# A new place for the pool of W's rows, and a new place in the queue for later weight loads, in attention followed by two MLPs

## The chip, the cores and the metric

The kernel runs on one core of a Trainium2 chip. The metric is the device time of one execution in microseconds (us), the median over several runs. A core has TensorE for matmuls (PE in the profile, its weight loads are PEld), VectorE (DVE), ScalarE (ACT), GpSimd (POOL) and SyncE (SP). Each works through its own queue of instructions in order. Here SP issues all loads and nearly all stores, in the order of its queue, and POOL issues a few accumulating transfers.

## The reference

```python
# q, k, v: (2, 12, 448, 64), causal attention, then
x = attention.transpose(0, 2, 1, 3).reshape(896, 768)
h = ((x @ w1) * (x @ w2)) @ w3          # w1, w2: 768 x 1024, w3: 1024 x 1024
y = h @ w_out                           # w_out: 1024 x 768
z = np.maximum(y @ w_in2, 0.0) ** 2     # w_in2: 768 x 2048
return z @ w_out2                       # w_out2: 2048 x 768
```

The weights come as 64-bit floats: the kernel loads both 32-bit words of each and joins them to a float32 on the chip. q, k and v are float32.

## The kernel before

**Stages.** Twelve head pairs of attention run first. Between their steps TensorE also computes W = w3 @ w_out (both operands are known, so the product with h becomes one product with W), in eight row blocks of 128 x 768 in two passes (`w_half`). The tiles that hold these eight blocks are `wraw`, tagged W0 to W7, in the pool `attw`. When the second pass has added its part to a block (L430 or L434 on VectorE), SP stores it to the DRAM tensor `w_dram` (L620); the last store is that of W7. W is read back from there about 80 us later. Then come the products with w1 and w2, with W, and the second MLP, each by Strassen's method at one level with seven products in the order 1, 2, 6, 5, 7, 3, 4 for two pairs P and Q of weight blocks. One product is 9 matmuls of 128 x 448. Every operand is split into a high and a low float32r part: ScalarE casts the high one (L437), VectorE subtracts (L430).

**The blocks of x.** Attention's result gives seven block sums of x: B11 and B22 (kept in the long-lived pool `big`), B21, T4, T1, T2, T3. The last five are tiles of the pool `xt`, which opens when attention's pools close. Their parts are made in the order B21, T2, T1, T3, T4. Product 1 reads B11, product 2 B21, product 6 T2, product 5 T1, product 7 T3, product 3 B22, product 4 T4. In the profile's names, numbers are left out: xB is any of B11, B22, B21, and xT any of T1 to T4. After product 1 ScalarE copies its bank to a second one (`bank<-bank`), and product 2 goes on adding in the first, so product 2 of a pair waits for that copy of its own pair.

**Where tiles lie.** Pools lie one behind the other in SBUF in the order in which they are opened. Attention's pools, and what each takes per partition: `rawb` 6,144 bytes; `attq` 10,752 (three tiles of q and k); `attw` 24,576 (eight rows of 3,072); `ringb` 24,576 (four tiles of 6,144, parts of w_out); `attc` 22,784 (the identity 512, the mask 1,792, `pt_all` 12,288, two tiles of w3 of 4,096); `att` 20,864. When they close, `xt` and then `big2` are opened on the same bytes with `reuse_waits="tile"`: a new tile waits for whoever last used an old tile on its bytes. `xt` holds, from its start, P5 (3,072) and then B21, T4, T1, T2, T3 of 10,752 each. `big2` starts at byte 56,832 of the region.

**The order of the work.** Every operation is added to a `Program` with what it must come after (`after`), what it must only be issued behind (`behind`), and estimated times for its engine. `Program.order` plays these forward: each engine takes, among the operations that could begin first, the one that is due first. The resulting order is emitted as it is, each engine then runs its queue in order, and waits between engines are real semaphores. Loads are chained (`turn="loads"`), so they keep their own order.

**Weight loads.** `load_raw` adds a load into a raw buffer. Weights of w1 and w2 are 128 x 768 with two words (768 KB) and alternate between two raw buffers. A buffer is free again when three instructions have read it: `prelu` on ScalarE (L494), `lower` (L498) and `join` (L502) on VectorE. The keys in `order` are those of w3 and w_out; the first four other loads are w1's and w2's blocks 0 and 1, then blocks 2 of both, and so on.

Of the kernel before, what the change touches and what calls it, by code (L numbers as in the profile page):

```python
# [124 lines left out]
def attention_moe_moe2(ctx: ExitStack, tc: tile.TileContext, qk, v, w1, w2, w3, w_out, w_in2, w_out2, out):  # L125
    nc = tc.nc
    NP_ALL, P, S2 = qk.shape
    S = S2 // 2
# [19 lines left out]
    CLOSE = 4  # L148
    LENT = (("wout", 2), ("wout", 3))
    PAUSE = 64  # L150
    big = ctx.enter_context(tc.tile_pool(name="big", bufs=1))
    rawp = ctx.enter_context(tc.tile_pool(name="raw", bufs=2))
    ps_w = ctx.enter_context(tc.tile_pool(name="ps_w", bufs=2, space=PSUM))

    w_dram = tc.dram_tile([KF // 2, 2, P, DM], F32, name="w_dram")
# [15 lines left out]
    def mm(o, l, r, start, stop, **more):  # L171
        return nc.tensor.matmul(o, l, r, start=start, stop=stop, **more)  # L172
# [4 lines left out]
    def load(key, pool, tag, cols=None):  # L177
        src = source[key[0]][key[1]]
        n = src.shape[-1]
        if key not in raws:  # L180
            t = pool.tile([P, DM, 2], U32, tag=tag, name=f"raw_{key[0]}_{key[1]}")
            raws[key] = t[:, :n]
        x, src = raws[key], src.bitcast(U32)
        if cols is not None:
            x, src = x[:, cols], src[:, 2 * cols.start:2 * cols.stop]
        nc.sync.dma_start(out=x.rearrange("p f w -> p (f w)"), in_=src)
# [58 lines left out]
    def wide(u):  # L245
        return u[0] == "H"
# [32 lines left out]
    for u in units:  # L279
        key = u if wide(u) else u[1]  # L280
# [23 lines left out]
    loads = [it for it in items if it[0] in source]  # L304
# [5 lines left out]
    order = []  # L310
    for g in range(N3 // KF):
# [7 lines left out]
    attention = ExitStack()  # L319
    rawb = attention.enter_context(tc.tile_pool(name="rawb", bufs=1))  # L320
    attq = attention.enter_context(tc.tile_pool(name="attq", bufs=2))
    attw = attention.enter_context(tc.tile_pool(name="attw", bufs=1))
    ringb = attention.enter_context(tc.tile_pool(name="ringb", bufs=4))
    attc = attention.enter_context(tc.tile_pool(name="attc", bufs=1))
    att = attention.enter_context(tc.tile_pool(name="att", bufs=2))
    ps_a = attention.enter_context(tc.tile_pool(name="ps_a", bufs=6, space=PSUM))
    wraw = [attw.tile([P, DM], F32, tag=f"W{i}", name=f"wraw{i}") for i in range(KF)]
    ident = attc.tile([P, P], F32, tag="ident", name="ident")
# [5 lines left out]
        out=mask, in_=mask, compare_op=ALU.is_ge, fill=MASKED,  # L334
# [4 lines left out]
    prog = Program({"S": 700})  # L339
# [3 lines left out]
    def act(width, psum=False, strided=False):  # L343
        gap = 60 + 0.815 * width if psum else 75 + (0.96 if strided else 0.845) * width
        return {"A": (gap, gap + 105)}

    def dve(width, fast=False):
        gap = 70 + (0.52 if fast else 1.038) * width
        return {"V": (gap, gap + 85)}
# [79 lines left out]
    def tt(out, x, y, what):  # L429
        return lambda e: engine_of[e].tensor_tensor(out(), x(), y(), op=what)  # L430

    def negated(out, x, y, what):

        return lambda e: nc.vector.scalar_tensor_tensor(out(), x(), -1.0, y(), op0=ALU.mult, op1=what)  # L434

    def copy(out, x):
        return lambda e: engine_of[e].copy(out(), x()) if e == "A" else engine_of[e].tensor_copy(out(), x())  # L437
# [22 lines left out]
    def turn(what, n):  # L460

        count[what] += 1
        return (count[what] - 1) % n

    def load_raw(key, cols=None):

        if cols is not None and key in raw_place:
            place = raw_place[key]
        elif key in LENT:
            place = ("ringb", turn("lent", 4))  # L470
        elif key in order and turn("plain", RAW) == RAW - 1:
            place = ("rawb", 0)
        else:
            place = ("raw", turn("raw", 2))
        width = source[key[0]][key[1]].shape[-1]
        if cols is not None:
            raw_place[key] = place
            words = [place + (s, cols.start // HN) for s in "hl"]
            width = cols.stop - cols.start
        else:  # L480
            words = [place + (s, c) for s in "hl" for c in range(2)]
        size = width / DM
        pool, tag = {"raw": (rawp, "raw"), "rawb": (rawb, "rawb"), "ringb": (ringb, "ringb")}[place[0]]
        prog.add({"S": (2200 * size, 2500 + 2200 * size)}, lambda e: load(key, pool, tag, cols), [], words, turn="loads")
        return words[:len(words) // 2], words[len(words) // 2:]

    raw_place = {}

    def float32(key, words, width, y, names, cols=slice(None)):

        high, low = words

        def prelu(e):
            nc.scalar.activation(y(), raws[key][:, cols, 1].bitcast(F32), AF.Prelu, scale=2.0 ** -112, alpha=-2.0 ** 32)  # L494

        def lower(e):
            x = raws[key][:, cols, 0]
            nc.vector.tensor_scalar(x, x, 2.0 ** -29, 7.0, ALU.mult, ALU.min)  # L498

        def join(e):  # L500
            yi = y().bitcast(U32)
            nc.vector.scalar_tensor_tensor(  # L502
                yi, yi, 3, raws[key][:, cols, 0], op0=ALU.logical_shift_left, op1=ALU.bitwise_or)

        prog.add(act(width, strided=True), prelu, high, names)
        prog.add(dve(width, fast=True), lower, low, low)
        prog.add(dve(width), join, [*low, *names], names)
# [49 lines left out]
    def w_columns(f, c):  # L557

        if (f, c) in w_halves:
            return  # L560
        cols, row = slice(c * HN, (c + 1) * HN), 2 + f
        w_halves[f, c] = [("xs", row, c)]
        words = load_raw(("wout", f), cols)
        float32(("wout", f), words, HN, lambda: xs[:, row, cols], w_halves[f, c], cols)
# [9 lines left out]
    def w_parts(key):  # L574

        kind, n = key
        if kind == "w3":
            return [w3t[n][:, s] for s in range(2)]
        return ring_pair(2 * n) if n < NB else [hls[key][:, s] for s in range(2)]

    def w_half(g, i, n):
        n3, cols = g * KF + i, slice(n * HN, (n + 1) * HN)
        plain = n3 < PLAIN
        if plain:
            w_row(("w3", n3))
            for f in range(NB):
                w_columns(f, n)
        else:
            for key in order[:order.index(("w3", n3)) + 1] + [("wout", g * NB + f) for f in range(NB)]:
                w_row(key)  # L590
        place, acc = turn("w", 2), []
        reads = list(w_rows["w3", n3])
        for f in range(NB):
            reads += w_halves[f, n] if plain else w_rows["wout", g * NB + f]

        def run(e):
            acc.append(ps_w.tile([P, HN], F32, tag="w", name=f"w{n3}_{n}"))
            for f in range(NB):
                c = slice(f * P, (f + 1) * P)
                if plain:  # L600
                    mm(acc[0], w3t[n3][:, 0, c].bitcast(F32), xs[:, 2 + f, cols], f == 0, f == NB - 1)
                    continue
                t, wo = w_parts(("w3", n3)), w_parts(("wout", g * NB + f))
                for s, r in ((0, 0), (0, 1), (1, 0)):
                    mm(acc[0], t[s][:, c], wo[r][:, n],
                       f == 0 and (s, r) == (0, 0), f == NB - 1 and (s, r) == (1, 0))

        t0 = (3.72 if plain else 3) * NB * HN * PE_ROW + 100
        prog.add({"T": (t0, t0 + 170)}, run, reads, [("w", place)])
        dst = wraw[i][:, cols]  # L610
        if g == 0:
            prog.add(dve(HN) | act(HN, True), copy(lambda: dst, lambda: acc[0]), [("w", place)], [("wraw", i, n)])
            return
        if n == 0:
            add = negated(lambda: dst, lambda: acc[0], lambda: dst, ALU.subtract)
        else:
            add = tt(lambda: dst, lambda: acc[0], lambda: dst, ALU.add)
        prog.add(dve(HN), add, [("w", place), ("wraw", i, n)], [("wraw", i, n)])
        if n == 1:
            prog.add({"S": (1200, 3000)}, lambda e: nc.sync.dma_start(out=w_dram[i // 2, i % 2], in_=wraw[i]),  # L620
                     [("wraw", i, 0), ("wraw", i, 1)], [("wdram", i)])

# [206 lines left out]
    def fill(n=1):  # L831
        for _ in range(n):
            w_half(*w_units.pop(0))
# [59 lines left out]
    def slot_in(n, k):  # L893
        return {"T1": 0, "T3": KH, "T2": 2 * KH, "B21": 3 * KH}[n] + k

    for n in ("B21", "T2", "T1", "T3"):
        for k in range(KH):
            i = slot_in(n, k)
# [3 lines left out]
    for k in range(KH):  # L902
        i, b = slot_in("T2", k), slot_in("B21", k)
# [223 lines left out]
    def product(n, pair, unit, first_of_all):  # L1127
# [21 lines left out]
        def run(e):  # L1149
            o = bank(i)  # L1150
            if first_of_all:
                x = t[0][:, :P].bitcast(F32)
                mm(o[:, :PAUSE], x, x[:, :PAUSE], True, True)
            for k in range(KH):
# [285 lines left out]
```

## Time and profile before

| | us |
|---|---|
| median of 3 runs | 526.03 |
| lowest, highest | 525.83, 527.21 |
| the profiled execution, its own time | 526.13 |
| its span, first to last instruction | 524.4 |
| TensorE, VectorE, ScalarE busy in it | 511.9, 481.1, 396.0 |
| mean granted clock of TensorE | 0.995 of full speed |

The span is shorter than the time of the same execution, because the time also holds what lies around the first and the last instruction. All positions in the trace are counted from the span's start. A granted clock of 1.00 is 2.4 GHz, 0.50 is 1.2 GHz.

### The profile page before, as it was taken

How to read it: one execution, taken by the hardware profiler on the slowest of the kernel's cores; microseconds unless marked ns; L12 is line 12 of the kernel's file. 1: busy time of each engine (PE TensorE's matmuls, PEld its weight loads, DVE VectorE, ACT ScalarE, POOL GpSimd, SP SyncE). 2: the span in 40 equal slices, each digit the busy share in tenths (PEclk: the TensorE clock that was granted, in tenths of full speed). 3: DMA queues.
4: the chain of work that ended last, by engine and by line, in shares of the span. 5: the costliest groups of instructions: out<-in, count | busy, mean ns of one | idle time of the engine just before them, and what ended most of it. 6: DMA issues, size and time to landing. Idle time of an engine off the chain costs nothing.

```text
span 524.4 us, 8532 instructions
## 1 busy us (share of the span) xinstructions
PE 511.9 (98%) x2901; PEld 463.4 (88%) x2901; DVE 481.1 (92%) x1148; ACT 396.0 (76%) x977; POOL 16.0 (3%) x24
## 2 busy tenths in 40 slices
PE   6999999999998999999999999999999999999996
PEld 5768888888887999999999999999999999998996
DVE  4999999998888999999875899999999999999996
ACT  5898888776858574737576578998999589959971
POOL 1000000000000011221100000000000000000000
PEclk9999999999998999999999999999999999999999
DMA  8764635553570479999672311504540454035114
GB/s 311 281 218 164 222 141 175 168 162 114 200 239 3 164 225 258 278 259 229 139 223 93 121 60 56 187 1 156 173 154 1 151 184 147 2 131 177 55 60 151
DMA packets 27339, 81.68 MB, mean 156 GB/s; under 512 B 2464, under 2 KB 13472, under 8 KB 27296
## 3 DMA queue, kind: packets, MB, share of 16 engines
q1 hardware_dynamic: 23520, 75.64, 42.4%
q0 software_dynamic: 3776, 5.51, 6.4%
q8 instruction: 23, 0.38, 0.3%
q14 instruction: 20, 0.16, 0.1%
HBM read 75.24 MB, written 14.55 MB: 171 GB/s over the span
## 4 chain that ended last, share of the span: by engine, by line
PE 80%; DVE 11%; DMA 5%; ACT 3%; issue 1%; DVEq 0%
PE bank L172 59%; PE w L172 10%; PE s L172 4%; DVE ring L430 3%; PE x L172 3%; PE pp L742 2%; DVE g L430 2%; DVE xs L502 2%; DMA w_dram<-wraw 1%; DVE p L727 1%; DMA raw_w<-in_w 1%; DMA raw_wout<-in_w_out 1%; DMA raw_win<-in_w_in 1%; PE ph L760 1%; DVE xs L430 1%
## 5 line engine op out<-in xcount | busy, mean ns | idle before, releaser
L172 PE MATMUL bank<-xT,ring 128*128 128x448 f32 x630 | 132.1, 366 | 0.0
L437 ACT CAST ring<-xs 128x384 fp32r<-128x384 f32 (+1 forms) x194 | 102.4, 545 | 37.7 <-DVE xs L430 15.3
L172 PEld LDWEIGHTS bank<-xT,ring 128*128 128x128 f32 x630 | 117.8, 188 | 9.3 <-ACT bank L437 0.2
L430 DVE TENSOR_TENSOR ring<-xs,ring 128x384 fp32r<-128x384 f32 (+1 forms) x194 | 112.4, 596 | 11.9 <-ACT ring L437 11.4
L172 PE MATMUL bank<-xB,ring 128*128 128x448 f32 x489 | 104.5, 370 | 3.0 <-ACT bank L437 2.8
L172 PE MATMUL bank<-ring,g 128*128 128x384 f32 x600 | 105.0, 335 | 0.0
L172 PEld LDWEIGHTS bank<-ring,g 128*128 128x128 f32 x600 | 104.1, 188 | 0.4 <-ACT bank L437 0.2
L172 PEld LDWEIGHTS bank<-xB,ring 128*128 128x128 f32 x489 | 92.8, 190 | 11.5 <-ACT bank L437 3.2
L710 ACT ACTIVATE p<-p,st 128x320 f32<-128x320 f32 (+3 forms) x96 | 48.2, 517 | 8.4 <-DVE st L700 8.4
L430 DVE TENSOR_TENSOR xs<-xs 128x384 f32<-128x384 f32 x96 | 52.3, 557 | 0.2
L700 DVE CUSTOM_DVE_ANT_0 p<-s,mask 128x320 f32<-128x320 f32 (+3 forms) x96 | 35.1, 423 | 6.9 <-PE s L172 6.9
L437 ACT CAST g<-fs 128x384 fp32r<-128x384 f32 (+1 forms) x88 | 35.4, 416 | 7.8 <-DVE fs L430 7.6
L430 DVE TENSOR_TENSOR g<-fs,g 128x384 fp32r<-128x384 f32 (+1 forms) x88 | 37.1, 436 | 0.7 <-ACT g L437 0.5
L172 PE MATMUL w<-hl_wout,w 128*128 128x384 f32 x192 | 36.3, 341 | 0.0
L494 ACT ACTIVATE xs<-raw_w 128x768 f32<-128x768 f32 (+1 forms) x30 | 24.2, 811 | 13.2 <-DMA raw_w<-in_w 6.9
L172 PEld LDWEIGHTS w<-hl_wout,w 128*128 128x128 f32 x192 | 33.0, 188 | 0.6
L437 ACT COPY fs<-bank 128x448 f32<-128x448 f32 (+1 forms) x52 | 27.5, 529 | 6.7 <-PE bank L172 6.6
L172 PE MATMUL s<-qk 64*128 64x448 f32 (+3 forms) x192 | 28.1, 440 | 4.0 <-DMA qk<-in_qk 4.0
L172 PE MATMUL bank<-ab,ring 128*128 128x448 f32 x144 | 29.5, 365 | 0.0
L172 PEld LDWEIGHTS bank<-ab,ring 128*128 128x128 f32 x144 | 27.1, 188 | 2.1
L172 PEld LDWEIGHTS s<-qk 64*128 64x128 f32 x192 | 17.5, 208 | 12.3 <-issue 6.1
L172 PE MATMUL w<-ring,w 128*128 128x384 f32 x144 | 27.4, 341 | 0.2 <-DVE wraw L437 0.2
(84 smaller groups left out, 692.1 us busy)
## 6 DMA issues: line engine op xcount, KB each, us to landing
raw_wout<-in_w_out SPq DMA_DIRECT2D x20, 768.0 KB, 4.4
raw_w<-in_w SPq DMA_DIRECT2D x16, 768.0 KB, 5.1
raw_win<-in_w_in SPq DMA_DIRECT2D x16, 768.0 KB, 4.3
raw_w<-in_w SPq DMA_DIRECT2D x16, 512.0 KB, 3.6
qk<-in_qk SPq DMA_DIRECT2D x12, 448.0 KB, 5.3
s_dram<-w_dram POOLq DMA_DIRECT2D x8, 576.0 KB, 8.9
v<-in_v SPq DMA_DIRECT2D x12, 256.0 KB, 3.0
raw_wout<-in_w_out SPq DMA_DIRECT2D x8, 384.0 KB, 6.9
```

The lines of the kernel that those rows point to most:

```text
L172: return nc.tensor.matmul(o, l, r, start=start, stop=stop, **more)
L430: return lambda e: engine_of[e].tensor_tensor(out(), x(), y(), op=what)
L437: return lambda e: engine_of[e].copy(out(), x()) if e == "A" else engine_of[e].tensor_copy(out(), x())
L494: nc.scalar.activation(y(), raws[key][:, cols, 1].bitcast(F32), AF.Prelu, scale=2.0 ** -112, alpha=-2.0 ** 32)
L502: nc.vector.scalar_tensor_tensor(yi, yi, 3, raws[key][:, cols, 0], op0=ALU.logical_shift_left, op1=ALU.bitwise_or)
L700: prog.add({"V": (gap, gap + 160)}, lambda e: nc.vector.tensor_tensor_reduce(block(p, j, i), s_t[p, j, g][:, o:o + w], mask[:, S - w:], QS ...
L710: prog.add({"A": (gap, gap + 100)}, lambda e, i=i: nc.scalar.activation(block(p, j, i), block(p, j, i), AF.Exp, bias=st_t[p][:, 0, j, i:i ...
L727: lambda e, i=i: nc.vector.tensor_scalar(block(p, j, i), block(p, j, i), st_t[p][:, 3, j, i:i + 1], None, ALU.mult),
L742: nc.tensor.transpose(x[0][:, o:o + P], block(p, j, i)[:, c * P:(c + 1) * P], ident)
L760: nc.tensor.transpose(x[0][:SHORT, o:o + SHORT], block(p, j, c)[SHORT:, c * P:c * P + SHORT], ident[SHORT:, SHORT:])
```

## The change

`attw` is opened as the last of attention's pools instead of the third, so `ringb`, `attc` and `att` move down by its 24,576 bytes, and it lies behind them. And of the loads of weights that are not w3's or w_out's, those from the fifth on may only be issued behind the last store of W. The first four stay as free as they were. Nothing that is computed changes.

```diff
+    EARLY = 4
...
     attq = attention.enter_context(tc.tile_pool(name="attq", bufs=2))
-    attw = attention.enter_context(tc.tile_pool(name="attw", bufs=1))
     ringb = attention.enter_context(tc.tile_pool(name="ringb", bufs=4))
     attc = attention.enter_context(tc.tile_pool(name="attc", bufs=1))
     att = attention.enter_context(tc.tile_pool(name="att", bufs=2))
+
+    attw = attention.enter_context(tc.tile_pool(name="attw", bufs=1))
...
-        prog.add({"S": (2200 * size, 2500 + 2200 * size)}, lambda e: load(key, pool, tag, cols), [], words, turn="loads")
+        if key not in order:
+            later.append(key)
+        prog.add({"S": (2200 * size, 2500 + 2200 * size)}, lambda e: load(key, pool, tag, cols), [], words,
+                 behind=stored[-1:] if len(later) > EARLY else [], turn="loads")
...
+    stored, later = [], []
...
         if n == 1:
-            prog.add({"S": (1200, 3000)}, lambda e: nc.sync.dma_start(out=w_dram[i // 2, i % 2], in_=wraw[i]),
-                     [("wraw", i, 0), ("wraw", i, 1)], [("wdram", i)])
+            stored.append(prog.add(
+                {"S": (1200, 3000)}, lambda e: nc.sync.dma_start(out=w_dram[i // 2, i % 2], in_=wraw[i]),
+                [("wraw", i, 0), ("wraw", i, 1)], [("wdram", i)]))
```

All stores of W are added before the first load of w1, so `stored[-1:]` is always the store of W7.

## Rows read from the trace of the kernel before

**Rows 1.** The page's first line, and busy time by engine.
```profile
span 524.4 us, 8532 instructions
PE 511.9 (98%) x2901; PEld 463.4 (88%) x2901; DVE 481.1 (92%) x1148; ACT 396.0 (76%) x977; POOL 16.0 (3%) x24
```

**Rows 2.** Chain that ended last, in order of time: start, length, what.
```profile
151.18 6.81 DMA w_dram<-wraw
...
159.53 266.53 PE bank L172 x1353
```

**Rows 3.** TensorE in order of time, 149.5 to 200: start, length, what, idle before.
```profile
150.27 1.95 PE L172 MATMUL x<-pt_all,v 128*64 128x448 f32 x16
...
152.60 4.10 PE L172 MATMUL bank<-xB,ring 128*128 128x448 f32 x19
159.53 5.48 PE L172 MATMUL bank<-xB,ring 128*128 128x448 f32 x18 [2.83 <-ACT bank L437]
164.84 11.11 PE L172 MATMUL bank<-xT,ring 128*128 128x448 f32 x54
175.79 3.81 PE L172 MATMUL bank<-xB,ring 128*128 128x448 f32 x18
```

**Rows 4.** ScalarE in order of time, 149.5 to 161.
```profile
152.70 1.50 ACT L437 CAST xB<-fs 128x448 fp32r<-128x448 f32 x3
158.01 1.03 ACT L437 CAST xT<-fs 128x448 fp32r<-128x448 f32 x2 [3.81 <-DMA w_dram<-wraw]
158.95 0.52 ACT L437 COPY bank<-bank 128x448 f32<-128x448 f32 x1
```

**Rows 5.** Windows of 1 us: length, PE, PEld, DVE, ACT, POOL; clock; DMA share, GB/s.
```profile
157.00:158.00 1.00, 0.00 (x0) 0.00 (x0) 0.00 (x0) 0.00 (x0) 0.00 (x0) 1.00 0.07 28
...
160.00:161.00 1.00, 1.00 (x5) 0.91 (x5) 1.00 (x2) 1.00 (x3) 0.00 (x0) 0.76 0.00 0
161.00:162.00 1.00, 1.00 (x4) 0.87 (x4) 0.82 (x3) 1.00 (x3) 0.00 (x0) 0.50 0.00 0
162.00:163.00 1.00, 1.00 (x5) 0.87 (x4) 1.00 (x3) 1.00 (x3) 0.00 (x0) 0.50 0.00 0
163.00:164.00 1.00, 1.00 (x4) 0.91 (x3) 1.00 (x3) 1.00 (x4) 0.00 (x0) 0.54 0.02 8
164.00:165.00 1.00, 1.00 (x6) 0.93 (x6) 1.00 (x4) 1.00 (x4) 0.00 (x0) 1.00 0.00 0
```

**Rows 6.** VectorE in order of time, 149.5 to 161.
```profile
150.60 0.55 DVE L430 TENSOR_TENSOR wraw<-w,wraw 128x384 f32<-128x384 f32 x1
...
153.87 1.69 DVE L430 TENSOR_TENSOR xB<-fs,xB 128x448 fp32r<-128x448 f32 x3
158.61 1.16 DVE L430 TENSOR_TENSOR xT<-fs,xT 128x448 fp32r<-128x448 f32 x2 [3.04 <-ACT xT L437]
```

**Rows 7.** SP's issues in order of time, 143 to 180.
```profile
146.43 4.13 SPq L186 DMA_DIRECT2D raw_w<-in_w  x2
151.18 0.33 SPq L620 DMA_DIRECT2D w_dram<-wraw  x1
173.29 2.82 SPq L186 DMA_DIRECT2D raw_w<-in_w  x2
```

**Rows 8.** Landing of the two loads issued at 146.4 and 150.2, by tile.
```profile
DMA to landing us min/median/max: 6.1/6.4/6.8
```

**Rows 9.** Landing of the first seven stores of W, by tile.
```profile
DMA to landing us min/median/max: 2.3/2.9/4.7
```

**Rows 10.** ScalarE in order of time, 163 to 178: its next reads of a raw buffer.
```profile
164.79 0.91 ACT L494 ACTIVATE xs<-raw_w 128x768 f32<-128x768 f32 x1
...
170.36 0.92 ACT L494 ACTIVATE xs<-raw_w 128x768 f32<-128x768 f32 x1
```

**Rows 11.** Windows as in rows 5, the stages after attention.
```profile
160.00:200.00 40.00, 40.00 (x191) 36.92 (x191) 39.08 (x73) 28.65 (x56) 1.72 (x2) 0.96 0.49 154
...
250.00:300.00 50.00, 50.00 (x248) 46.35 (x247) 37.54 (x57) 30.88 (x52) 2.08 (x2) 1.00 0.51 147
```

## The prediction, made before the changed kernel was run

> **What bounds the kernel now.** I read the page first: TensorE is busy for 98% of the span [rows 1], so a change can only pay where TensorE stands still or runs slowly. Then the chain that ended last, because it names the places where something else has the lead. One such place lies just where attention ends: the chain goes through the last store of W, and from 159.53 on through TensorE alone for 266.53 us [rows 2]. So whatever moves TensorE's start at 159.53 moves 266 us of work behind it. Third, the engines one by one around that place. TensorE ends P's and Q's product 1 at 152.60 + 4.10 = 156.70 and stands idle for 2.83 us, until ScalarE's copy of a bank [rows 3]. That copy isn't late by itself: on ScalarE it stands behind two casts of T2, and these waited 3.81 us for the store of W7 [rows 4]. B21's three casts just ahead did not wait. Last, windows of one microsecond. After the idle stretch the granted clock falls to 0.76, 0.50, 0.50, 0.54 between 160 and 164 and is back at 1.00 after it [rows 5]; 0.50 is the 1.2 GHz level.
>
> **Why a cast of x waits for a store of W.** This comes from the sizes of the pools. Before, `attw` begins at 6,144 + 10,752 = 16,896, so W6 and W7 take bytes 35,328 to 41,472. In `xt`, T2 begins at 3,072 + 3 x 10,752 = 35,328. T2's first bytes are thus those of W6 and W7, and T2 is the first of the T blocks that is made. The trace agrees: the casts that wait are the first xT ones, and they start 0.02 us after the store landed at 151.18 + 6.81 = 157.99 [rows 2, 4].
>
> **Part one, the pool.** After the change, the region reads: `rawb` to 6,144, `attq` to 16,896, `ringb` to 41,472, `attc` to 64,256, `att` to 85,120, `attw` to 109,696. T2 (35,328 to 46,080) then covers the last `ringb` tile, the identity, the mask and 2,304 bytes of `pt_all`. Of these `pt_all` is used longest: by attention's last matmuls, which end at 150.27 + 1.95 = 152.22 [rows 3]. ScalarE is done with B21 only at 152.70 + 1.50 = 154.20 [rows 4]. So the new wait is over 2 us before ScalarE could start anyway; its price is zero, and it would count only if those matmuls ended after 154.2. T3 covers `pt_all` and the start of a w3 tile, T1 and T4 mostly `ringb`: all of them are read by TensorE ahead of 152.22 too. W's rows now lie under `big2`, at 85,120 - 56,832 = 28,288 and up within it, behind its first 7,168 and 21,504 bytes. What is written there are results of later products, of w2 among them, tens of us after the store has landed. I price that at zero too.
>
> **What TensorE gets.** In rows 4 the first bank copy starts 0.94 us after the first T2 cast. From 154.20 that gives 155.14, and with its 0.52 us the copy is done at 155.66, a microsecond before 156.70. The 2.83 us go. VectorE follows: it ends B21's low parts at 153.87 + 1.69 = 155.56 and can go on with T2 at once, where it waited for 3.04 us [rows 6]. Three low parts at about 0.6 us are done by 157.4, and T2 is wanted only after two more products, at about 156.70 + 3.64 = 160.3. No new wait there.
>
> The clock is the second term. The 18 matmuls from 159.53 took 5.48 us; the 18 of the same form at 175.79 took 3.81 [rows 3]. That is 1.67 us, and the windows give the same another way: 0.24 + 0.50 + 0.50 + 0.46 = 1.70 [rows 5]. In this trace the fall comes right behind the idle stretch, so I take it to go with it; its lower bound is zero, if the fall had another cause.
>
> **Part two, the loads.** Two loads, the fifth and sixth of w1 and w2, are issued at 146.43 and 150.2, ahead of the store at 151.18 [rows 7]. Now they are issued behind it, at about 151.5 and 151.9; their buffers are free by then. The store waits in SP's queue for VectorE's last sum, which ends at 151.15 [rows 6], so it is not issued earlier than now. But it no longer has 1.5 MB ahead of it: it lands after something like the other seven's 2.3 to 4.7 us [rows 9] instead of 6.81. With part one nobody waits for it, so this is worth nothing by itself. It is a second cure for the same stall.
>
> The cost: the loads land later. Together they and the store are the same three transfers as before, of which none took longer than 6.8 us [rows 2, 8]; so at most about 158.7. ScalarE reads them at 164.79 and 170.36 [rows 10], which become 160.3 and 165.9 if all moves by 4.5. The cover is 1.6 us for the first and 7 for the second. From above, if store and loads ran strictly one after the other, 4.7 + 6.8 = 11.5 us would put the first at 163.0, and ScalarE would stand for 2.7 us in front of copies out of banks. I take the nearer row, the same three transfers, and price it at zero. SP has nothing else queued until 173.29 [rows 7], so no other transfer is held up, and no load of attention is touched.
>
> The planner sees one new edge. Loads five and six are planned some 6 us later, still ahead of the moment when their data is taken; so I expect the same order on TensorE, VectorE and ScalarE, and on SP three transfers in another order.
>
> The Trainium skill speaks against this part: in "DMA: Bandwidth & Descriptors", section "Rules for kernel authors", it says to issue a transfer early and to wait for it late. By it the loads moved behind the store lose 5 and 2 us of lead, and the sum would fall by whatever of that is not covered. The rows give 1.6 us of cover at the tightest place, so here the rule would cost nothing.
>
> **Sum.** -2.83 - 1.67 + 0 + 0 = -4.50 us. The profiled execution took 526.13 us, 1.73 more than its span; 526.13 - 4.50 = 521.63. It lies 0.10 above the median of the runs, so I forecast **521.5**. Does it last to the end? Behind 159.53 TensorE never waits until 426, and VectorE and the loads take their pace from TensorE by way of buffers; VectorE has 12.5 us of idle time between 250 and 300 to fall in step [rows 11].
>
> **Rivals.** *VectorE keeps the rest.* It is busy for 39.08 of 40 us after 160 [rows 11], and it gains only 3.05 us (158.61 to 155.56) against TensorE's 4.50. If TensorE has less than 1.45 us of lead to spare over VectorE's data, the gain is 3.05: 523.0. Against it: TensorE shows no wait for VectorE there, even where it comes back to full clock. 8%.
>
> *The clock falls anyway*, since the cause was not the idle stretch: -2.83, 523.2. Against it is only the order of events. 5%.
>
> *The pool doesn't move T2 off W*, because tiles are not placed in the order I read from the code. Then part two decides. The store lands at 153.5 to 155.9 by rows 9; TensorE starts 1.52 us after it (158.01 to 159.53), so it idles for 0 to 0.7 us: 521.5 to 522.2. The skill's rule on completion (the same page, "Queues, rings and completion order": a transfer's semaphore is written only after every earlier write of that DMA engine) agrees with 6.81 against 2.3 to 4.7 and would by itself move the store the same way. 5%.
>
> *No change*, if some tile other than W7 ends T2's wait equally late, such as a load still landing under it: 526.0. I see none in the sizes. 3%.
>
> *Slower: the fifth load comes late.* ScalarE waits in order at its read, and copies out of banks stand behind it. Each microsecond past 160.3 costs TensorE at most one. To lose more than the gain and 1.6 us besides it would have to land after 166.4, 15 us after its issue; the longest of the two was 6.8 [rows 8]. At 12 us it would only eat 3 of the 4.5. If the planner also puts other work behind it, 528. 3%.
>
> **How the numbers follow.** The forecast holds 76%; its own spread is some 0.7 us, from the margins above. The two cases at 523.0 and 523.2 and the late load that eats part of the gain set the upper end, 523.3; below, the gain cannot be much over 4.5, and 520.7 allows for small shifts in the order behind. A measurement of this kernel tells 0.3%, 1.6 us, from no change. Faster: 76 + 8 + 5 + 5 = 94, of which I leave 1 for what I don't see: 93%. Within 0.3%: 4%. Slower: 3%.
>
> **What would show it.** Right: the first xT cast starts at about 154.2 with no wait for the store; TensorE has no gap at 156.70 and the clock stays at 1.00 through 165; T2's first product starts at about 160.3 instead of 164.84; the store is issued ahead of both loads and lands within 4.7 us; the chain no longer holds `w_dram<-wraw`. Wrong: a wait of ScalarE for `raw_w` near 160, a gap of TensorE that VectorE ends between 160 and 200, or a gain at 165 that is gone again by 426.

## The result, and the profile after

The changed kernel takes 522.05 us (median of 6 runs, 521.29 to 522.85); the kernel before took 526.59 in the same comparison (6 runs). The ratio is 0.991, with a 95% interval of 0.989 to 0.9931. 4.54 us were gained where 4.50 had been worked out, and 522.05 lies within the range given. The profiled execution of the changed kernel is the longest of its six, 522.85; the last section tells of a reason.

In the page, the span is shorter by 3.4 us and the work of the engines is the same:
```profile
span 521.0 us, 8529 instructions
PE 511.3 (98%) x2901; PEld 461.7 (89%) x2901; DVE 481.4 (92%) x1148; ACT 395.8 (76%) x977; POOL 15.9 (3%) x24
```
In the chain that ended last, nothing stands any more between attention's last matmuls and TensorE's own long stretch. The store of W, 6.81 us of the chain before [rows 2], is gone from it:
```profile
149.81 1.88 PE x L173 x16
151.69 281.88 PE bank L173 x1428
```
TensorE and then ScalarE in order of time. All starts in this execution lie about 0.5 us earlier already ahead of the place in question (152.06 against 152.60), so distances count:
```profile
152.06 7.75 PE L173 MATMUL bank<-xB,ring 128*128 128x448 f32 x37
159.65 11.11 PE L173 MATMUL bank<-xT,ring 128*128 128x448 f32 x54
```
```profile
152.16 1.50 ACT L439 CAST xB<-fs 128x448 fp32r<-128x448 f32 x3
153.56 1.04 ACT L439 CAST xT<-fs 128x448 fp32r<-128x448 f32 x2
154.50 0.53 ACT L439 COPY bank<-bank 128x448 f32<-128x448 f32 x1
...
160.35 0.90 ACT L501 ACTIVATE xs<-raw_w 128x768 f32<-128x768 f32 x1
...
165.17 0.92 ACT L501 ACTIVATE xs<-raw_w 128x768 f32<-128x768 f32 x1
```
The two groups of 19 and 18 matmuls of [rows 3] have become one of 37 without a gap. T2's first product starts 159.65 - 152.06 = 7.59 us behind the start of that group; before, it was 164.84 - 152.60 = 12.24. So 4.65 us are gained at this place: 1.66 because the 18 matmuls ahead of T2 take 3.65 us instead of 5.31 (159.53 to 164.84), and 2.99 because the first of them no longer stands. That is 0.16 more than the idle time of 2.83 in the row, which counts from the modelled end of the matmul before it. T2's casts follow B21's directly, with no wait behind them, and the bank copy starts 0.94 us after the first of them, as in [rows 4].

Windows of 1 us, columns as in [rows 5]. The clock stays at full speed:
```profile
157.00:158.00 1.00, 1.00 (x6) 0.93 (x5) 1.00 (x3) 1.00 (x3) 0.00 (x0) 1.00 0.14 55
160.00:161.00 1.00, 1.00 (x7) 0.93 (x6) 1.00 (x3) 1.00 (x3) 0.00 (x0) 1.00 0.00 0
161.00:162.00 1.00, 1.00 (x7) 0.93 (x6) 1.00 (x3) 1.00 (x3) 0.00 (x0) 1.00 0.00 0
```
SP's issues, then the landing of the store of W7 and of the two loads behind it. Two stores follow each other (145.03 and, 5.6 us later, 150.63), and the loads come behind:
```profile
145.03 5.93 SPq L628 DMA_DIRECT2D w_dram<-wraw  x2
151.06 27.46 SPq L187 DMA_DIRECT2D raw_w<-in_w  x6
```
```profile
DMA to landing us min/median/max: 2.6/2.6/2.6
```
```profile
DMA to landing us min/median/max: 5.0/5.7/6.3
```
The store lands at 153.25 instead of 157.99, and the loads at 156.03 and 157.88, some 4.3 and 7.3 us ahead of ScalarE's reads at 160.35 and 165.17.

### The profile page after: what moved, and what is told of

Read it like the earlier page. It is cut to its first block, busy times and chain, and to the rows that moved or that the text cites. A ratio compares the mean times of both kernels' runs of the same rounds, so it can differ in the third digit from the quotient of the medians.

```text
span 521.0 us, 8529 instructions
## 1 busy us (share of the span) xinstructions
PE 511.3 (98%) x2901; PEld 461.7 (89%) x2901; DVE 481.4 (92%) x1148; ACT 395.8 (76%) x977; POOL 15.9 (3%) x24
## 4 chain that ended last, share of the span: by engine, by line
PE 87%; DVE 7%; ACT 4%; DMA 2%; issue 0%; DVEq 0%
PE bank L173 62%; PE w L173 13%; PE s L173 4%; PE x L173 4%; PE pp L750 3%; DVE ring L432 2%; DVE g L432 2%; ACT p L718 2%; PE ph L768 1%; DMA raw_win<-in_w_in 1%; DVE xs L509 1%; DMA qk<-in_qk 1%; DVE xs L432 1%; ACT ring L439 0%; ACT g L439 0%; DVE p L735 0%
## 5 line engine op out<-in xcount | busy, mean ns | idle before, releaser
L173 PE MATMUL bank<-xB,ring 128*128 128x448 f32 x489 | 103.3, 367 | 0.2
L173 PEld LDWEIGHTS bank<-xB,ring 128*128 128x128 f32 x489 | 91.5, 188 | 8.8 <-DVE ring L432 0.5
```

## The experiments

The theory: T2 lies over W6 and W7, so T2's casts wait for the store of W7, and TensorE idles and slows down behind them. Either part of the change ends that, and the loads behind the store cost nothing as long as their cover lasts. The rivals: the order of the loads alone does it, or the pool alone; the slow clock has another cause; loads issued later cost time.

| run | median us | before, same comparison | ratio, 95% interval | from the first xB group to the first xT product, us |
|---|---|---|---|---|
| again (changed kernel) | 523.30 | 527.34 | 0.9917, 0.9894 to 0.9940 | 7.58 |
| pool_only | 522.36 | 527.34 | 0.9904, 0.9889 to 0.9919 | 7.58 |
| loads_only | 521.99 | 527.34 | 0.9905, 0.9886 to 0.9925 | 7.59 |
| rows_reversed | 521.66 | 527.34 | 0.9893, 0.9879 to 0.9906 | 7.59 |
| filler | 525.98 | 527.05 | 0.9973, 0.9946 to 0.9999 | 10.45 |
| pad_before | 530.83 | 527.05 | 1.0076, 1.0049 to 1.0103 | 14.91 |
| pad_after | 521.90 | 527.05 | 0.9928, 0.9901 to 0.9954 | 7.58 |
| pad_pool | 522.29 | 526.65 | 0.9921, 0.9891 to 0.9951 | 7.59 |
| early2 | 527.78 | 527.05 | 1.0024, 1.0001 to 1.0046 | 10.12 |
| early3 | 526.79 | 526.65 | 0.9992, 0.9972 to 1.0011 | 7.59 |

The last column is from each run's own trace: the start of TensorE's first `xT` row less that of the row that begins at 152.60 in [rows 3], where the kernel before has 12.24.

**again.** The changed kernel once more.

> The changed kernel once more. Theory: 4.5 us under the kernel before (about 522.1 against 526.6), TensorE without a gap between 156 and 160, clock 1.00 there. On the slower matmul cadence that the changed kernel's profile shows between 233 and 326 (207 ns from start to start against 203 in the kernel before): if it belongs to one execution, its place or length differs here; if it belongs to the program, it comes at the same place.

The gain repeats: 4.0 us between the medians, and 7.58 us at the place in question. The slower cadence came at another place, so its place belongs to the execution; see the last section.

**pool_only.** The pool moved, the loads left as they were.
```diff
-    attw = attention.enter_context(tc.tile_pool(name="attw", bufs=1))
     ringb = attention.enter_context(tc.tile_pool(name="ringb", bufs=4))
...
+    attw = attention.enter_context(tc.tile_pool(name="attw", bufs=1))
     ps_a = attention.enter_context(tc.tile_pool(name="ps_a", bufs=6, space=PSUM))
```


> The pool of W's rows laid out last, the loads as before. Theory (T2's bytes were those of W7): the store still lands some 6.8 us after its issue, behind both loads, but no cast waits for it; TensorE has no gap; the whole gain, about 522.1. Rival (the order of the loads is what cures): the gap of 2.8 us and the low clock stay, 526.6.

The landing of W7's store and ScalarE in order of time:
```profile
DMA to landing us min/median/max: 6.9/6.9/6.9
```
```profile
152.31 1.50 ACT L437 CAST xB<-fs 128x448 fp32r<-128x448 f32 x3
153.72 1.04 ACT L437 CAST xT<-fs 128x448 fp32r<-128x448 f32 x2
```
The store is as slow as before, and T2's casts start 4 us ahead of its landing at 157.7. So the wait was one for bytes, and the pool alone gives the whole gain.

**loads_only.** The loads behind the store, the pool left in third place (the second hunk of the change alone).

> The loads behind the last store, the pool where it was. Theory: T2 still waits for the store of W7, but the store lands 2.3 to 4.7 us after its issue at about 151, at 153.3 to 155.9, and ScalarE is free for T2 at about 154; TensorE loses 0 to 0.7 us: 522.1 to 522.8. Rival (the pool alone cures): the cast waits as long as before, 526.6.

```profile
DMA to landing us min/median/max: 2.6/2.6/2.6
```
```profile
152.67 1.50 ACT L438 CAST xB<-fs 128x448 fp32r<-128x448 f32 x3
154.07 1.04 ACT L438 CAST xT<-fs 128x448 fp32r<-128x448 f32 x2
```
T2 still lies over W7, but the store was issued at 151.14 and landed at 153.70, 0.37 us before ScalarE was free for T2. This too gives the whole gain, with 0.37 us to spare at the casts. The two parts are two cures of one stall; the gain is not their sum. The Trainium skill's "DMA: Bandwidth & Descriptors", section "Queues, rings and completion order", says that a transfer's semaphore is written only after every earlier write of that DMA engine; the trace agrees, with 2.6 us for the store ahead of the loads and 6.9 behind them, though it doesn't single this cause out.

**rows_reversed.** The kernel before, with the row tiles of W laid out in reverse.
```diff
-    wraw = [attw.tile([P, DM], F32, tag=f"W{i}", name=f"wraw{i}") for i in range(KF)]
+    wraw = [attw.tile([P, DM], F32, tag=f"W{i}", name=f"wraw{i}") for i in reversed(range(KF))][::-1]
```


> The pool where it was, the loads as before, but the eight row tiles of W laid out in reverse, so that T2 lies over W0 and W1, stored some 45 us earlier, and T4 over W7 and W6. T4 is made last, some 11 us behind T2. Theory (single tiles matter): no wait, about 522.1. Rival (new tiles wait for the whole pool of W's rows, or the place of that pool is what counts): 526.6.

The landing of the store of W7:
```profile
DMA to landing us min/median/max: 6.6/6.6/6.6
```
521.66 us: neither pool nor loads have moved, the store, issued at 150.71, still lands only at 157.35, and the gain is there. So what counts is which row lies under T2, not the place of the pool. W7 and W6 now lie under T4, which is made some 10 us later than T2: its first cast starts at 163.01, after the landing.

**filler.** The stall is kept, and TensorE gets something to do in it.
```diff
+    FILL = 14
...
+    def filler(unit, i):
+        def run(e):
+            for _ in range(FILL):
+                mm(bank(i), hls[unit][0][:, :P], xB["B11"][:, 0, 0], True, True)
+
+        prog.add({"T": (0, 0)}, run)
...
+        if at == 2:
+            filler(plan[0][3][0], free_banks[1])
         if kind == "product":
```


> The kernel before, with 14 extra matmuls of 128 x 448 into a bank that nobody uses yet, between Q's product 1 and P's product 2 (their result is never read). They fill TensorE's idle 2.83 us at about 0.2 us each and leave the wait as it is. Theory (the clock falls because of the idle stretch): the clock stays at 1.00 behind it and the 18 matmuls take 3.8 us instead of 5.5, so 1.7 us less than before, about 524.9. Rival (the clock falls for another reason): 526.6 or a little more.

ScalarE, TensorE, and one window:
```profile
157.79 1.04 ACT L438 CAST xT<-fs 128x448 fp32r<-128x448 f32 x2 [3.57 <-DMA w_dram<-wraw]
```
```profile
152.61 10.61 PE L173 MATMUL bank<-xB,ring 128*128 128x448 f32 x51
163.06 11.10 PE L173 MATMUL bank<-xT,ring 128*128 128x448 f32 x54
```
```profile
161.00:162.00 1.00, 1.00 (x6) 0.87 (x6) 0.82 (x2) 1.00 (x4) 0.00 (x0) 1.00 0.00 0
```
The wait for the store is there as before, TensorE has no gap, and the clock, 0.50 in this window before [rows 5], is 1.00. The distance to T2's product falls from 12.24 to 10.45 us, by 1.79. Of this the 18 matmuls ahead of it are 1.63: they take 3.68 us from start to start instead of 5.31, with 1.67 to 1.70 forecast. The rest goes with the store, which landed 0.2 us earlier in this execution, so that ScalarE waited for 3.57 us instead of 3.81. The medians differ by 1.1 us with an interval of 0.05 to 2.8, which holds it without pinning it down. What remains to 7.59, 2.86 us, is the time of the 14 extra matmuls.

The clocks of all executions say more than the medians. The four windows of [rows 5] lack 1.70 us at full clock, 0.003 of the span; so an execution with this fall can't show a mean granted clock above 0.997. Of the kernel before's 63 executions in the three later comparisons, 28 show 0.998 or more: these did not have it, or not in full. Of filler's 12 all show 0.998 or more. In the comparison with filler, the 18 of the kernel before with 0.998 or more have a median of 526.12 us, close to filler's 525.98; the other 17 have 528.06. So the fall goes with the idle stretch, but at most 35 of the 63 executions with that stretch paid for it.

**pad_before.** The kernel before, with one more load ahead of the last store.
```diff
+    padp = attention.enter_context(tc.tile_pool(name="padp", bufs=1))
...
+    def store(i):
+        if i == KF - 1:
+            pad = padp.tile([P, 1024], U32, tag="pad", name="pad")
+            nc.sync.dma_start(out=pad, in_=w2[KF - 1].bitcast(U32)[:, :1024])
+        nc.sync.dma_start(out=w_dram[i // 2, i % 2], in_=wraw[i])
...
-            prog.add({"S": (1200, 3000)}, lambda e: nc.sync.dma_start(out=w_dram[i // 2, i % 2], in_=wraw[i]),
+            prog.add({"S": (1200, 3000)}, lambda e: store(i),
```


> The kernel before with one more load of 512 KB, into a tile that nobody reads, issued just ahead of the store of W7. Theory: the store lands later by about 2 us (512 KB at the 250 GB/s of the loads around it), T2's casts and TensorE with it: 528 to 529. Rival (the store's landing isn't what TensorE waits for): 526.6.

ScalarE and TensorE:
```profile
159.72 1.03 ACT L438 CAST xT<-fs 128x448 fp32r<-128x448 f32 x2 [5.79 <-DMA w_dram<-wraw]
```
```profile
161.23 6.17 PE L172 MATMUL bank<-xB,ring 128*128 128x448 f32 x18 [4.81 <-ACT bank L438]
...
218.88 2.09 PE L172 MATMUL bank<-xB,ring 128*128 128x448 f32 x9 [1.05 <-ACT bank L438]
```
The store takes 8.8 us, TensorE's stall grows by 1.98 us and the slow matmuls behind it by 0.69: 2.67 at this place; the 2 expected had left the clock's part out. The median is 3.8 above the kernel before, where 1.4 to 2.4 were expected; the second row shows another wait, 1.05 us at 218.88, which the kernel before does not have there. All 12 executions show a mean granted clock of 0.997 or less, where the kernel before has such clocks in 17 of 35; if the longer stall is always followed by the fall, that is another part of the difference.

**pad_after.** The changed kernel with the same extra load.

> The changed kernel with the same extra load of 512 KB just ahead of the store of W7. Theory: the store lands later and nobody waits for it, and the fifth load lands later by about 2 us, against the cover of 1.6 at its read by ScalarE as it was forecast (4.3 as the changed kernel's profile has it): 522.1, at most 522.6. Rival (TensorE still hangs on the store): 523.5 or more.

521.90, but this run was no test: with loads five and six out of the way, SP came to the extra load at 145.67, and it landed at 150.27, before the store was issued. The store took 2.6 us as without it.

**pad_pool.** The test that this was meant to be, on pool_only.

> The pool of W's rows last, the loads as before, and the same extra load of 512 KB just ahead of the store of W7, now behind the fifth and sixth load as in the run of the kernel before with it (in the changed kernel with it, the extra load went out 5 us earlier and landed before the store was issued). Theory: the store lands at about 159.7 as there, and nobody waits for it: TensorE has no gap, 522.1 to 522.6. Rival (TensorE still hangs on the store): 528 or more.

The landing of the store, and ScalarE:
```profile
DMA to landing us min/median/max: 9.4/9.4/9.4
```
```profile
152.70 1.50 ACT L438 CAST xB<-fs 128x448 fp32r<-128x448 f32 x3
154.10 1.03 ACT L438 CAST xT<-fs 128x448 fp32r<-128x448 f32 x2
```
The store lands at 160.6, later than ever, 6.5 us after the casts that used to wait for it, and the kernel takes 522.29 us. The next transfer that reads `w_dram` is issued at 179.10 (sums made within DRAM), so the late landing delays nobody there either. What cost 3.8 us over the old layout costs nothing over the new one.

**early2.** Four loads behind the store instead of two (`EARLY = 2`).

> The changed kernel with EARLY = 2: the third and fourth load of w1 and w2 also go behind the last store. They then land at about 156 to 158 instead of 140 and 147, and product 6 needs sums of what they bring at about 159.6. Theory (loads behind the store are free only as long as their cover lasts): ScalarE waits for raw_w, TensorE waits 1 to 4 us before product 6, and 1 to 5 us of the gain are given back: 523 to 527. Rival (the place of loads in the queue doesn't matter here): 522.1.

TensorE in order of time:
```profile
161.69 11.78 PE L173 MATMUL bank<-xT,ring 128*128 128x448 f32 x54 [2.37 <-ACT ring L439]
...
238.26 5.49 PE L173 MATMUL bank<-xB,ring 128*128 128x448 f32 x18 [2.19 <-ACT bank L439]
```
The whole gain is gone, and a little more: 527.78. Product 6 waits 2.37 us for its sums. ScalarE did not wait for `raw_w`, as had been expected: its reads at 156.33 and 158.52 follow the work before them directly, and it is VectorE that is behind, busy for 4.96 of the 5 us from 157 with what the late loads bring among other work. Another wait of 2.19 us, with slow matmuls behind it, comes 77 us later.

**early3.** Only the fourth load joins the two (`EARLY = 3`).

> The changed kernel with EARLY = 3: only the fourth load joins those behind the last store. It brings Q's second block, whose sums product 6 of Q needs one product later than P's, at about 161.5. Theory: it lands at about 155, its chain on VectorE (lower, join, two sums, low part, some 3.5 us among other work) ends at about 160 to 162: 0 to 1.5 us given back there, 522.1 to 523.6. Rival (any of the first four loads behind the store costs as much as two of them): 527 to 528.

```profile
162.91 9.59 PE L173 MATMUL bank<-xT,ring 128*128 128x448 f32 x45 [0.92 <-ACT ring L439]
...
210.58 2.08 PE L173 MATMUL bank<-xB,ring 128*128 128x448 f32 x9 [1.40 <-ACT bank L439]
213.45 2.12 PE L173 MATMUL bank<-xB,ring 128*128 128x448 f32 x9 [0.79 <-ACT bank L439]
```
526.79, nearly as much as early2 and not the 522.1 to 523.6 expected. The wait at the place itself is 0.92 us, as worked out; but two more of 2.2 us together follow at 210, where the changed kernel's profile shows none above 0.1 and its repeat 0.6 together. VectorE, busy for 18.00 of 18 and 20.00 of 20 us from 157 to 195 in this run, can't make up work that starts later; but it is as busy in the changed kernel, 18.00 and 19.82. Its order differs in this run too, because the planner knows of the late load. And in this trace the slower cadence of the last section runs from about 214 to 338, some 600 matmuls at 4 ns, or 2.4 us beside the 3.1 us of waits. How much of the loss is backlog, order or cadence stays open.

With both runs, the rival of late loads is real, and the limit lies between the fourth load and the fifth. The Trainium skill's rule to issue transfers early (the same page, section "Rules for kernel authors") had been priced at nothing for loads five and six; there the trace bears the price out, and one load further, going against the rule costs the whole gain.

## Why the prediction was right, step by step

**The wait for bytes.** Right, and shown from both sides: other bytes under T2 (pool_only, rows_reversed) or an earlier landing (loads_only) end it, a later landing lengthens it (pad_before) only where T2 lies over W7 (pad_pool).

**The idle term**, -2.83: 2.99 at the place; the row's idle time, counted from a modelled end, was 0.16 too small a price. **The clock term**, -1.67 with a lower bound of zero: 1.66 at the place and 1.63 by filler, and the low clock went with the idle stretch. Together 4.65 us at the place against 4.50.

**The total** came out closer than the working deserves. The forecast took the clock term from one profiled execution and charged it in full, but at most 35 of 63 executions of the kernel before paid it. 2.99 with that share of 1.66 is at most some 3.9 us on average, an estimate from these counts (the clocks of the six executions behind 526.59 are not on record); 4.54 lie between the medians. The difference of some 0.6 us isn't explained by what happens at the place. So the agreement of 4.54 with 4.50 is partly luck, while the mechanism and the two prices at the place are shown.

**The loads.** They landed within 6.3 us as expected, on the same side of ScalarE's reads. Their cover was 4.3 and 7.3 us, not 1.6 and 7: the first was bounded by the slowest landing.

**The planner.** The step "I expect the same order on TensorE, VectorE and ScalarE" was wrong in part. TensorE's order is the same. VectorE's differs from the kernel before between 212 and 246, a couple of dozen instructions standing in another place, and ScalarE's in one. No time shows in it: pool_only, whose order is that of before throughout, is as fast.

**Does it last?** Not fully, and the rival that VectorE would keep part had a grain of truth. "Behind 159.53 TensorE never waits" is no longer so near 210 in most traces of the faster kernels. TensorE, VectorE and ScalarE of pool_only there:
```profile
204.21 5.74 PE L172 MATMUL bank<-xB,ring 128*128 128x448 f32 x27
210.58 2.09 PE L172 MATMUL bank<-xB,ring 128*128 128x448 f32 x9 [0.64 <-ACT bank L437]
```
```profile
207.06 0.57 DVE L498 TENSOR_SCALAR raw_w<-raw_w 128x768 uint32<-128x768 uint32 x1 [0.88 <-DMA raw_w<-in_w]
207.54 0.95 DVE L502 SCALAR_TENSOR_TENSOR xs<-xs,raw_w 128x768 uint32<-128x768 uint32 x1
208.41 0.56 DVE L430 TENSOR_TENSOR ring<-xs,ring 128x384 fp32r<-128x384 f32 x1
208.88 0.62 DVE L434 SCALAR_TENSOR_TENSOR ab<-bank,fs 128x448 f32<-128x448 f32 x1
```
```profile
209.53 0.57 ACT L437 CAST ab<-ab 128x448 fp32r<-128x448 f32 x1 [2.05 <-DVE ab L434]
210.00 0.53 ACT L437 COPY bank<-bank 128x448 f32<-128x448 f32 x1
```
Read from below: TensorE waits for a bank copy, which stands behind a cast, which waits for VectorE, which waited 0.88 us for a load that took 6.5 us to land; in the changed kernel's profile the same load took 5.5, and TensorE waited less than 0.1 us. That is the reading of one trace. In again, loads_only, rows_reversed and pad_pool the same load took only 4.0 to 4.5 us, and TensorE still waited 0.3 to 0.6 us there in all; in pad_after it took 4.5, and TensorE waited less than 0.1. So the landing of this load alone doesn't set the wait, and what does stays open. It is small against 4.65.

None of the versions beats the changed kernel beyond its interval; rows_reversed does the same with one line.

## What to carry to other kernels

When tiles of a new stage are laid over those of an old one, the place of each tile is a dependency: put under the tile that is needed first what is free first, and under the one needed last what a slow transfer still reads. A stall at such a seam can also cost what the clock loses behind it, in the profiled execution 1.66 us on 2.99, but not in every execution. And before a load is moved behind something, count who needs it next: two loads moved for nothing here, and with a third the whole gain was gone.

## What the runs showed that had not been expected

**Two cadences of the same matmuls at full clock.** In these traces matmuls of 128 x 448 follow each other, wherever TensorE doesn't wait, in one of two ways: 202.7 ns apart on average, or 206.7. The kernel before, then the changed kernel, at the two ends of the same 414 matmuls:
```profile
241.65 11.11 PE L172 MATMUL bank<-xT,ring 128*128 128x448 f32 x54
...
325.55 3.81 PE L172 MATMUL bank<-xT,ring 128*128 128x448 f32 x18
```
```profile
236.55 11.32 PE L173 MATMUL bank<-xT,ring 128*128 128x448 f32 x54
...
322.11 3.88 PE L173 MATMUL bank<-xT,ring 128*128 128x448 f32 x18
```
83.90 us against 85.56, 1.66 us more for the same work, with TensorE busy throughout. In this execution the slower cadence began near 233 and lasted until the matmuls of this width end, near 333. In again it ran from about 184 to 210, in pool_only from 182 to 209, in pad_before from 167 to 217, in early2 from 165 to 185, and in filler and early3 from 214 to 338; in loads_only, rows_reversed, pad_after and pad_pool no such stretch is seen between 160 and 320. So its place belongs to an execution (again and the changed kernel are one program), and it accounts for much of why the changed kernel's span is shorter by 3.4 us only. In again, pool_only and pad_before it ends at a wait of TensorE; in filler, early2 and early3 it begins soon behind one, and here it begins without one. What starts it isn't shown.

**The length of an idle stretch alone doesn't decide on the clock.** In early2, TensorE idles for 2.37 us ahead of 161.69, and the clock stays at 1.00; it idles for 2.19 us ahead of 238.26, and the clock falls:
```profile
160.00:161.00 1.00, 0.00 (x0) 0.00 (x0) 1.00 (x3) 1.00 (x3) 0.00 (x0) 1.00 0.98 375
...
163.00:164.00 1.00, 1.00 (x7) 0.93 (x6) 1.00 (x3) 0.41 (x1) 0.00 (x0) 1.00 0.94 381
```
```profile
239.00:240.00 1.00, 1.00 (x6) 0.90 (x5) 1.00 (x3) 1.00 (x4) 0.67 (x1) 0.80 0.96 263
240.00:241.00 1.00, 1.00 (x4) 0.91 (x3) 1.00 (x3) 0.82 (x2) 0.00 (x0) 0.50 1.02 359
```
So a stall of this size has two prices, with and without the slow matmuls behind it, as the 28 of 63 executions of the kernel before without the fall say too. The forecast's lower bound of zero for that term was a sound one; its full price as the expected value was not.
